# Turning q and k in quarters of the array, and moving a quarter of one block's first product behind the block before it

## The chip, the cores and the metric

The kernel runs on one core of a Trainium2 chip. The metric is the device time of one execution in microseconds (us); a profile of one execution has its own span, which is a little shorter than the time. The engines are named as in the profile: PE is TensorE (PEld its weight loads), DVE is VectorE, ACT is ScalarE, POOL is GpSimd, SP is SyncE, which here only issues transfers.

## What is computed

A retention layer feeds a feed-forward block. From the reference, cut to its core:

```python
for t in range(S):                       # B=4, H=8, S=768, D=64
    state = gamma * state + k[:, :, t] (outer) v[:, :, t]
    y[:, :, t] = scale * q[:, :, t] @ state
x = y.transpose(0, 2, 1, 3).reshape(B * S, H * D)      # 3072 x 512
h = x @ w_in                                            # 512 x 2048
out = (h * sigmoid(1.702 * h)) @ w_out                  # 2048 x 512
```

All is float32, but the weights come in as 64-bit floats, seen by the kernel as pairs of 32-bit words. Turning them into float32 is a part of the work.

## The kernel before, in words

**Retention in chunks.** Time is cut into chunks of 64 steps for two batches at a time, which makes 24 chunks of 128 rows. `turn(j)` turns q and k of chunk j so that the head dimension lies on the partitions. For the first eight chunks it does so on TensorE, with matmuls against the identity (L232) into two PSUM tiles `pt` under the tag "y"; `turned(j)` copies these to SBUF on ACT (L243). For later chunks DVE transposes. `attend(j, f)` (the table calls it `step`) makes the scores of chunk j (L265, into `pa`), the update of the state of chunk f (L275, into `pa`) and the output of f (L284 from the state, L290 from the scores, into `py`). All these are matmuls of 64x64 on quarters of the array, in the order 00, 01, 10, 11 of row half and column half. DVE then does `masked` (L296: scores times mask), `by_state` (called `state` in the table, L301), `output` (`x`, L312) and `updated` (L330, L332); ACT does `decay` (L254) and `aged` (L322).

**The feed-forward block.** The 3072 rows are six blocks (NB) of 512 rows, that is four chunks each. The first product of a block, x by w_in, has 16 column groups of 128, handled as 8 pairs. The second product, by w_out, is `down(m)`: seven partial products (a scheme of the Strassen kind on 2 x 2 sub-blocks: seven products in place of eight, paid for with sums and differences of the operands), each in four units, so 28 units of four matmuls of 128x256 (L488). For blocks 2 to 5 the first product is done in seven as well: `up(d)`, d from 0 to 3, each seven products of four matmuls (L435). Blocks 0 and 1 come while the weights are still being converted, and use the plain eight: `up0(th, p)` for block 0 (eight matmuls of 128x256, L384) and `up1(f)` for block 1 (four matmuls of 128x512, L396). Each is followed by `gate` (a sigmoid on ACT, L356) and `gated` (a multiplication on DVE that frees the PSUM tile, L361).

**The weights.** `Narrow` converts one block of weights: `abs` on ACT (L189), `half` (three DVE operations, L193 to L195) and `rest` (three more, L199 to L204). Blocks 1 to 15 are 128x1024; block 0 is done as two of 128x512 (0a and 0b). Numbers 0 to 7 are w_in, pair by pair, and 8 to 15 are w_out. `fetch` loads them into one of three buffers that take turns (`w7a` and so on in the table). `sums_w2(p)` makes the sums of w_out that the seven products need (L415 to L417), `sums_w2_t3` one more (L420), `sums_w1` and `sums_x` those for `up`, on POOL; `sums_g` the sums of the hidden values (L424 to L426 on DVE, L427 on POOL) after each unit of the third partial product, which is key "y1" in the list `P_`. The fourth partial product reads what L426 writes.

**The order of the work.** TensorE is scheduled by hand: its queue is the order in which the program emits. For the front (blocks 0 and 1, chunks 0 to 7) this is a table of names written out in the kernel, from `k0 table q0` to `gated0.1.3`. Names such as `up0.1.3` and `gate1.5` mean block, row half and pair, or block and column group. `pin` keeps the table's order on the other engines as well; what is not pinned (the sums, for instance) goes where the scheduler puts it. Behind the table follows a loop over the blocks m: `up` for m > 1, then the 28 units of `down(m)`, with the chunks of a later block put `between` at every third unit. `ps` is the PSUM pool, with two buffers under each of the tags "x" and "y"; a unit can start only once the tile that held its buffer has been read.

X1 is the input of block 1. It lies in `W2[:, 6]`, the place that `sums_w2_t3` fills later. The hidden values of block 0 lie in the slots 4 to 6 of W1 and X that the sums for `up` write later.

Of the kernel before, what the change touches and what calls it, by code (L numbers as in the profile page):

```python
# [9 lines left out]
F32 = mybir.dt.float32  # L10
# [18 lines left out]
def kernel(  # L29
# [43 lines left out]
    NP = NFF // 2  # L73
    C4 = 32
    EH = DM // 2
    assert 2 * D == P and HP * P == DM and NC % CB == 0 and B % 2 == 0 and DM == 512 and NFF == 16

    const = ctx.enter_context(tc.tile_pool(name="const", bufs=1))
# [29 lines left out]
    def pin(i):  # L108
        return tc.keep_in_program_order(i) if ordered[0] else i
# [112 lines left out]
    def turn(j):  # L222

        QT[j], KT[j] = home(j, "qT"), home(j, "kT")
        if j < 2 * CB:

            x = QKV.pop(("q", j)), QKV["kn", j]
            TURNED[j] = p = [ps.tile([P, HP, P], F32, name="pt", tag="y") for i in range(2)]
            for n in (1, 0) if j else (0, 1):
                for s in range(HP):  # L230
                    for r in range(2):
                        pe.matmul(p[n][HALF[r], s, :], x[n][:, HP * r + s, :], ident, start=True, stop=True)  # L232
        else:
            for t, name in ((QT[j], "q"), (KT[j], "k")):
                tc.keep_in_program_order(dve.transpose(
                    t.rearrange("p h t -> p (h t)"), QKV.pop((name, j)).rearrange("p h s d -> p (h s d)")))
        if 2 * CB <= j < NCH - 2:
            load(j + 2, "qk")

    def turned(j):  # L240
        p = TURNED.pop(j)
# [148 lines left out]
    def up1(f):  # L390

        p, ab = divmod(f, 2)
        h = ps.tile([P, 2, TH], F32, name="ph", tag="xy"[f % 2])
        for c in range(4):
            w = W1[:, p, 2 * ab + c // 2, c % 2, :]
            pe.matmul(h, w, X1[:, c // 2:4:2, c % 2, :], start=(c == 0), stop=(c == 3))  # L396
        return G[:, p, ab:4:2, :], h


    def sums_w1(p):  # L400
        w = [W1[:, p:p + 2, s] for s in range(7)]
        pool.tensor_add(w[4], w[2], w[3])
        pool.tensor_sub(w[6], w[0], w[2])
        pool.tensor_sub(w[5], w[4], w[0])
        pool.tensor_sub(w[2], w[1], w[5])

    def sums_x():
        pool.tensor_sub(X[:, 4], X[:, 2], X[:, 0])
        pool.tensor_sub(X[:, 6], X[:, 3], X[:, 2])
        pool.tensor_sub(X[:, 5], X[:, 3], X[:, 4])  # L410
        pool.tensor_sub(X[:, 2], X[:, 1], X[:, 5])

    def sums_w2(p):
        w = [W2[:, s, p:p + 2, :] for s in range(7)]
        dve.tensor_sub(w[4], w[1], w[0])  # L415
        dve.tensor_sub(w[5], w[3], w[4])
        dve.tensor_sub(w[1], w[2], w[5])  # L417
# [48 lines left out]
    def down(m):  # L466
# [5 lines left out]

        def keep(name, tag, src):
            kept[name] = one.tile([P, 2, EH], F32, name=name, tag=tag)
            act.activation(kept[name], src, AF.Copy)  # L475

        def put(th, e, a, b):
            o = two.tile([P, 2, EH], F32, name="o")
            dve.tensor_add(o, a, b)  # L479
            (pool if m < NB - 1 else act).dma_start(rows[th, e], o)  # L480

        def part(key, sa, sb, new, last, d, then):
            if d == 0 and new:
                acc[key] = ps.tile([P, 2, EH], F32, name="pd", tag=key[0])
            p0 = acc[key]
            for p in range(2 * d, 2 * d + 2):
                for n in range(2):
                    pe.matmul(p0[:, n, :], g1(m, p, sa)[:, n * P:(n + 1) * P], W2[:, sb, p, :],  # L488
                              start=(new and p == 0 and n == 0), stop=(last and p == NP - 1), skip_group_check=True)
            if d == NP // 2 - 1:  # L490
                then(p0)
# [42 lines left out]
        dve.memset(ones, 1.0)  # L534
        dve.memset(first, 0.0)

    def keep_warm(n):

        for _ in range(n):
            pe.matmul(idle.rearrange("p (a b) -> p a b", a=4), ident, ident[:, None, :].to_broadcast([P, 4, P]),  # L540
                      start=True, stop=True)

    def rows():

# [20 lines left out]
    def late_loads():  # L565
# [10 lines left out]
        "warm2": lambda: keep_warm(2), "warm1": lambda: keep_warm(1)}  # L576
# [15 lines left out]
    units = [0]  # L592
# [17 lines left out]

    begin()
    for name in """
        k0 table q0 warm2 turn0 w0b rows warm1 k1 abs0b q1 turned0 step0 v0 w0a half0b mask turn1 causal
        rest0b masked0 decay0 v1 decay1 abs0a half0a step-0 updated0 turned1 q2 step1 rowd k2 whole w2b
        turn2 w2a x0 k3 aged1 masked1 turned2 v2 rest0a abs2 q3 step-1 updated1 state1 decay2 aged2 step2 q4
        x1 half2 decay3 w3b w3a up0.0.0 masked2 turn3 k4 step-2 v3 q5 rest2 k5 gate0.0.0 turned3 updated2
        gated0.0.0 state2 step3 up0.0.2 masked3 abs3 half3 x2 rest3 turn4 w1b step-3 aged3 gate0.0.2 turned4
        state3 w1a w5b updated3 v5 decay4 k6 abs1 x3 gated0.0.2 q6 turn5 half1 up0.0.3 turned5 up0.1.2 step4  # L620
        aged4 w5a rest1 v4 gate0.0.3 decay5 w6a masked4 turn6 gate0.1.2 abs5 w6b step5-4 gated0.0.3 half5
        rest5 up0.0.1 updated4 turned6 k7 abs6 gated0.1.2 state4 gate0.0.1 w4b up0.1.1 half6 aged5
        gated0.0.1 w8a up0.0.5 rest6 masked5 decay6 w4a q7 up0.1.5 gate0.1.1 x4 gate0.0.5 gated0.1.1
        gated0.0.5 abs4 step6-5 w8b half4 gate0.1.5 state5 updated5 turn7 turned7 aged6 abs8 w9b up0.1.6
        gate0.1.6 x5 v6 masked6 gated0.1.5 step7-6 v7 w9a decay7 up0.1.0 rest4 w7a masked7 abs9 updated6
        state6 x6 gated0.1.6 w7b half8 step-7 state7 up0.1.4 gate0.1.4 abs7 x7 up1.8 rest8 half7 up1.5
        gated0.1.4 gate1.8 gated1.8 w11a rest7 half9 up1.4 gate1.4 w10b gated1.4 w10a w11b up0.0.7 gate0.1.0
        up1.0 gated0.1.0 gate0.0.7 rest9 up1.3 gate1.0 gated1.0 abs10 gated0.0.7 w12a gate1.5 gate1.3 up1.2
        gated1.5 gated1.3 gate1.2 w12b up1.6 gated1.2 gate1.6 abs11 up1.9 gate1.9 half11 rest11 up1.11
        gated1.9 gated1.6 up0.0.4 up0.1.7 abs12 w14b half10 gate0.0.4 rest10 aged7 up0.0.6 gate1.11 updated7  # L630
        gated1.11 gated0.0.4 up1.10 gate0.1.7 w14a half12 gate0.0.6 gated0.1.7 abs14 half14 w13a gate1.10
        gated0.0.6 rest12 w13b up1.7 gate1.7 up1.12 up1.13 gated1.10 gate1.13 rest14 gated1.7 gated1.13
        abs13 half13 gate1.12 w15a up1.15 gate1.15 gated1.15 w15b late_loads up1.14 abs15 gated1.12 up0.1.3
        half15 rest13 rest15 up1.1 gate1.14 gated1.14 gate0.1.3 gate1.1 gated1.1 gated0.1.3
    """.split():
        works[name]()
    ordered[0] = False
# [5 lines left out]
    for m in range(NB):  # L643
        between = []
        if m == 0:
            between = [lambda: turn(2 * CB), lambda: step(2 * CB), lambda: None, lambda: None, lambda: turn(2 * CB + 1)]
        elif m == 1:
            between = [lambda: (decay(2 * CB), load(2 * CB + 1, "v"))] + chunks(2 * CB + 1, 3 * CB)[1:]
        elif 1 < m < NB - 2:
            between = chunks((m + 1) * CB + 1, (m + 2) * CB)  # L650
        elif m == NB - 2:
            between = chunks((m + 1) * CB + 1, NCH - 1) + [lambda: step(None, NCH - 1)]
        if m > 1:
            for d in range(NP // 2):
                up(d)
        for n, unit in enumerate(down(m)):
            unit()
            if m == 0 and n < NP and n % 2:
# [3 lines left out]
            if m == 1 and n % 8 == 3:  # L662
                sums_w1(n // 4)
            if between and n % 3 == 2:
                between.pop(0)()
# [48 lines left out]
```

## Time and profile before

| | |
|---|---|
| time, three runs | 684.38, 684.86, 684.91 us, median 684.86 |
| span of the profiled execution | 682.2 us |
| TensorE clock that was granted, of full speed | 0.999 |
| L488, second products of all blocks (1120, 160 and more records) | 381 to 382 ns each |
| L396, block 1's first product | 128 records, 55.6 us busy |
| L232, the turns | 256 records |
| transfers | 46.55 MB, 217 GB/s over the first 24 us |

A record of L488 is one of two that make up a float32 matmul. The durations of matmuls overlap, since they are pipelined: what one costs is the time from one start to the next. In the front (0 to 158 us) the weights are converted, chunks 0 to 7 are worked through, and both first products run. At 158.5 us the second product of block 0 starts, its third partial product at 173.2 us; the last matmul of the program ends at 678.4 us.

### The profile page before, as it was taken

To read this page: it belongs to the slowest core of one execution; us is meant where nothing else is said; L and a number is where in the kernel's file an instruction comes from. 1 tells how busy PE (TensorE), PEld (TensorE's weight loads), DVE (VectorE), ACT (ScalarE), POOL (GpSimd) and SP (SyncE) were. 2 spreads that over 40 slices of the span, in tenths; PEclk is the share of its full clock that TensorE was granted. 3 is DMA by queue.
4 is the path that set the end of the run, shared out by engine and by line. 5 is a ranking of instruction groups with operands and counts; after the bars stand their busy time and mean duration, and the time that the engine had idled before them with its cause. 6 is when DMAs were issued, how large, how long until landed. Compare 5 with 4: busy or idle time off the path is not lost.

```text
span 682.2 us, 13881 instructions
## 1 busy us (share of the span) xinstructions
PE 669.4 (98%) x5832; PEld 558.1 (82%) x5832; DVE 366.9 (54%) x513; ACT 150.9 (22%) x293; POOL 125.6 (18%) x116
## 2 busy tenths in 40 slices
PE   6899999999999999999999999999999999999997
PEld 4788854756888888888888888888888888888886
DVE  4899984989711843443653443563444372345241
ACT  5764423221000001332000332000333000233000
POOL 3000000000467414000434000245100243000020
PEclk9999999999999999999999999999999999999999
DMA  8886531332222224301333310323310210000001
GB/s 192 243 250 203 155 128 58 123 86 35 48 34 64 62 46 103 57 1 16 73 58 84 53 32 11 75 45 76 74 35 4 51 43 32 16 0 1 16 0 47
DMA packets 140318, 46.55 MB, mean 68 GB/s; under 512 B 131808, under 2 KB 132832, under 8 KB 140256
## 3 DMA queue, kind: packets, MB, share of 16 engines
q1 hardware_dynamic: 136352, 39.10, 24.7%
q0 software_dynamic: 1760, 5.26, 2.0%
q10 hardware_dynamic: 2144, 1.31, 0.6%
q8 instruction: 46, 0.75, 0.4%
q14 instruction: 16, 0.13, 0.1%
HBM read 39.33 MB, written 6.29 MB: 67 GB/s over the span
## 4 chain that ended last, share of the span: by engine, by line
PE 84%; DVE 7%; SPq 5%; DMA 1%; issue 1%; ACT 1%; ACTq 0%
PE pd L488 38%; PE px L435 16%; PE py L435 12%; PE ph L384 6%; SPq L140 4%; PE ph L396 4%; PE pa L265 2%; PE pt L232 2%; PE py L290 2%; PE pa L275 2%; PE py L284 2%; SPq L126 1%; DVE G L425 1%; DMA W<-in_moe_w_out_dram 1%; ACT G L254 1%
## 5 line engine op out<-in xcount | busy, mean ns | idle before, releaser
L488 PE MATMUL pd<-W,G 128*128 128x256 f32 x1120 | 247.4, 381 | 0.4 <-DVE G L426 0.3
L488 PEld LDWEIGHTS pd<-W,G 128*128 128x128 f32 x1120 | 211.3, 190 | 30.3 <-DVE G L426 1.2
L435 PE MATMUL px<-X,W 128*128 128x256 f32 x512 | 119.0, 379 | 0.0
L435 PEld LDWEIGHTS px<-X,W 128*128 128x128 f32 x512 | 97.3, 190 | 13.2
L435 PE MATMUL py<-X,W 128*128 128x256 f32 x384 | 90.7, 379 | 0.0
L435 PEld LDWEIGHTS py<-X,W 128*128 128x128 f32 x384 | 73.0, 190 | 9.9
L384 PE MATMUL ph<-X,W 128*128 128x256 f32 x256 | 57.6, 382 | 0.0
L396 PE MATMUL ph<-W,W 128*128 128x512 f32 x128 | 55.6, 592 | 0.0
L384 PEld LDWEIGHTS ph<-X,W 128*128 128x128 f32 x256 | 48.1, 190 | 8.2 <-issue 1.1
L256 POOL TENSOR_TENSOR kd<-kn_in,cold 128x512 f32<-128x512 f32 x14 | 16.4, 1169 | 186.2 <-PE pa L275 164.5
L396 PEld LDWEIGHTS ph<-W,W 128*128 128x128 f32 x128 | 24.3, 190 | 28.9 <-issue 28.4
L427 POOL TENSOR_TENSOR G<-G 128x512 f32<-128x512 f32 x20 | 29.5, 1482 | 91.8 <-DVE G L426 91.8
L356 ACT ACTIVATE sg<-G 128x512 f32<-128x512 f32 x48 | 30.3, 630 | 51.3 <-DVE G L445 31.0
L361 DVE TENSOR_TENSOR G<-G,sg 128x512 f32<-128x512 f32 x48 | 33.4, 695 | 13.7 <-ACT sg L356 13.7
L296 DVE TENSOR_TENSOR at<-pa,mask 128x512 f32<-128x512 f32 x16 | 11.0, 685 | 53.7 <-PE pa L275 53.7
L488 PE MATMUL pd<-W,W 128*128 128x256 f32 x160 | 35.9, 382 | 1.6 <-DVE G L361 1.3
L324 POOL TENSOR_TENSOR state<-state,whole 128x512 f32<-128x512 f32 x13 | 13.5, 1041 | 126.9 <-DVE state L332 126.7
L488 PEld LDWEIGHTS pd<-W,W 128*128 128x128 f32 x160 | 30.1, 190 | 7.2 <-DVE G L361 2.1
L356 ACT ACTIVATE sg<-ph 128x512 f32<-128x512 f32 x32 | 19.0, 596 | 73.4 <-PE ph L396 30.1
L475 ACT ACTIVATE u<-pd 128x512 f32<-128x512 f32 x6 | 3.6, 597 | 135.5 <-PE pd L488 135.5
L480 POOL DMA_DIRECT2D out_dram<-o x20 | 14.9, 746 | 94.3 <-DVE o L479 94.3
L445 DVE TENSOR_TENSOR G<-py,p 128x512 f32<-128x512 f32 x16 | 11.1, 691 | 38.1 <-PE py L435 38.1
(109 smaller groups left out, 661.9 us busy)
## 6 DMA issues: line engine op xcount, KB each, us to landing
W<-in_moe_w_in_dram SPq DMA_DIRECT2D x12, 512.0 KB, 5.0
v_in<-in_v_dram SPq DMA_DIRECT2D x48, 128.0 KB, 3.1
kn_in<-in_k_dram SPq DMA_DIRECT2D x42, 128.0 KB, 3.2
W<-in_moe_w_out_dram SPq DMA_DIRECT2D x10, 512.0 KB, 3.7
out_dram<-o POOLq DMA_DIRECT2D x20, 256.0 KB, 2.6
q_sq<-in_q_dram SPq DMA_DIRECT2D x256, 16.0 KB, 1.8
k_sq<-in_k_dram SPq DMA_DIRECT2D x256, 16.0 KB, 1.8
G<-in_moe_w_out_dram SPq DMA_DIRECT2D x6, 512.0 KB, 3.9
```

Source lines behind the costliest of these rows:

```text
L140: tc.keep_in_program_order(sp.dma_start(t[r0:r0 + C4, :, n], src[b + n * C4 // D, h0:h0 + HP, t0:t0 + C4, d0:d0 + C4] .rearrange("h p d -> ...
L232: pe.matmul(p[n][HALF[r], s, :], x[n][:, HP * r + s, :], ident, start=True, stop=True)
L256: pool.tensor_mul(KD[j], x, d.to_broadcast([P, H, D]))
L265: pe.matmul(pa[HALF[i], r, 0, s, :], KT[j][HALF[r], s, HALF[i]], QT[j][HALF[r], s, HALF[i]], start=True, stop=True)
L356: pin(act.activation(s, h, AF.Sigmoid, scale=1.702))
L361: pin(dve.tensor_mul(g, h[:, i], s[:, i]))
L384: pe.matmul(h[:, ab], w, X[:, 2 * th + c // 2, c % 2, :], start=(ab == 0 and c == 0), stop=(c == 3), skip_group_check=True)
L396: pe.matmul(h, w, X1[:, c // 2:4:2, c % 2, :], start=(c == 0), stop=(c == 3))
L427: pool.tensor_sub(a[1], a[1], a[0])
L435: pe.matmul(acc[:, u, :], W1[:, 2 * d + u, sa, c, :], X[:, sb, c, :], start=(start and u == 0 and c == 0), stop=(stop and c == 1), skip_gr ...
L480: (pool if m < NB - 1 else act).dma_start(rows[th, e], o)
L488: pe.matmul(p0[:, n, :], g1(m, p, sa)[:, n * P:(n + 1) * P], W2[:, sb, p, :], start=(new and p == 0 and n == 0), stop=(last and p == NP - ...
```

## The change

1. **Turns in quarters.** Each turn becomes 32 matmuls of 64x64 in place of 16 with 128 rows and 128 columns. The two PSUM tiles are now split by row half and not by q and k, so each copy holds a half of both.
2. **A quarter of block 1's first product moves.** MOVED = 1: `up1` is left for 12 of 16 column groups. The last four come after block 0's second product as one `up(3)`, in seven products. For this ACT copies X1 to X, and DVE does the sums for pair 3 and for X.
3. **The table reaches into block 0's second product.** Eight of its 28 units (`down`) and all four `sums_w2` stand in the table, which is written anew from the first to the last name. Once `down` has begun, first-product units take only tag "y".
4. **The end.** The last partial product of the last block is done one column half after the other (`last_part`), so that the first half is added and sent off while the second is still being multiplied.
5. `rows`, the product that spreads the decays, comes ahead of the two warm-up matmuls; a third one is gone.

The diff, cut to its core:

```diff
-            TURNED[j] = p = [ps.tile([P, HP, P], F32, name="pt", tag="y") for i in range(2)]
+            TURNED[j] = p = [ps.tile([P, 2, HP, D], F32, name="pt", tag="y") for i in range(2)]
             for n in (1, 0) if j else (0, 1):
                 for s in range(HP):
-                    for r in range(2):
-                        pe.matmul(p[n][HALF[r], s, :], x[n][:, HP * r + s, :], ident, start=True, stop=True)
+                    for i, r in TWO:
+                        pe.matmul(p[i][HALF[r], n, s, :], x[n][HALF[i], HP * r + s, :], ident[HALF[i], HALF[i]],
+                                  start=True, stop=True)
...
-        for n in (1, 0) if j else (0, 1):
-            pin(act.activation((QT[j], KT[j])[n], p[n], AF.Copy))
+        for i, p in enumerate(TURNED.pop(j)):
+            pin(act.activation(t[:, :, :, HALF[i]], p, AF.Copy))
...
+        def last_part(d, halves={}):
+            n = d // (NP // 4)
+            if d % (NP // 4) == 0:
+                halves[n] = ps.tile([P, EH], F32, name="pd", tag="xy"[n])
+            for p in range(NP // 2 * (d % 2), NP // 2 * (d % 2 + 1)):
+                pe.matmul(halves[n], g1(m, p, 1)[:, n * P:(n + 1) * P], W2[:, 3, p, :], start=(p == 0), stop=(p == NP - 1))
+            if d % 2:
+                o = two.tile([P, 2, EH], F32, name="o")
+                dve.tensor_add(o[:, 0], halves[n], kept["t"][:, n])
+                act.dma_start(rows[0, 1][:, n], o[:, 0])
...
-            args = *args, "x" if n < 3 else "xxyx"[(n - 3) % 4]
+            args = *args, "y" if downs else "x" if n < 3 else "xxyx"[(n - 3) % 4]
+        else:
+            args = *args, "y" if downs else "xy"[args[0] % 2]
...
-            + [(f"1.{f}", up1, f) for f in range(NFF)]:
+            + [(f"1.{f}", up1, f) for f in range(NFF - 4 * MOVED)]:
...
-        if m > 1:
+        if m == 1:
+            for d in range(NP // 2 - MOVED, NP // 2):
+                sums_w1(2 * d, dve)
+                if d == NP // 2 - MOVED:
+                    sums_x(dve)
+                up(d)
+        elif m > 1:
             for d in range(NP // 2):
                 up(d)
-        for n, unit in enumerate(down(m)):
+        for n, unit in enumerate(down(m) if m else second):
+            if m == 0 and n < len(downs):
+                continue
             unit()
-            if m == 0 and n < NP and n % 2:
-                sums_w2(n - 1)
             if m == 0 and NP <= n < 3 * NP // 2:
+                act.activation(X[:, n - NP], X1[:, n - NP], AF.Copy)
                 sums_w2_t3(2 * (n - NP))
```

The new table begins and ends so (a line of "..." stands for the part between):

```
w2a k0 table q0 w2b decay0 rows warm abs2 q1 k1 warm turn0 turned0 step0 mask half2 v0 rowd causal
...
gate0.0.4 w13b up1.9 w14a half12 abs13 gated0.0.4 w14b gate1.6 gate1.9 abs14 gated1.6 gate1.11
rest12 half13 up1.2 gated1.11 down up1.8 gated1.9 gate1.8 half14 w15b w15a late_loads rest14 abs15
down gated1.8 rest13 up0.1.6 half15 rest15 gate0.1.6 down updated7 gated0.1.6 sums1 up1.1 up1.5
gate1.1 sums0 gate1.5 sums3 down gated1.1 gated1.5 up1.7 down down gate1.7 down gated1.7 gate1.2
down sums2 gated1.2
```

More of the change, by code (lines that the diff above doesn't have):

```diff
@@ L75 @@
     EH = DM // 2
+    MOVED = 1
     assert 2 * D == P and HP * P == DM and NC % CB == 0 and B % 2 == 0 and DM == 512 and NFF == 16
@@ L240, in turned @@
     def turned(j):
[L241 to L243 removed]
+        t = G[:, 0:2, j % 2 * 2:j % 2 * 2 + 2, :].rearrange("p n a t -> p n (a t)").rearrange(
+            "p n (s t) -> p n s t", s=HP)
+        for i, p in enumerate(TURNED.pop(j)):
+            pin(act.activation(t[:, :, :, HALF[i]], p, AF.Copy))
     def decay(j):
@@ L388, in up0, with up1 @@
         return [(g1(0, p, 2 + i), i) for i in range(2)], h
-    def up1(f):
+    def up1(f, tag):
         p, ab = divmod(f, 2)
-        h = ps.tile([P, 2, TH], F32, name="ph", tag="xy"[f % 2])
+        h = ps.tile([P, 2, TH], F32, name="ph", tag=tag)
         for c in range(4):
@@ L397, in up1, with sums_w1, sums_x @@
         return G[:, p, ab:4:2, :], h
-    def sums_w1(p):
+    def sums_w1(p, by=pool):
         w = [W1[:, p:p + 2, s] for s in range(7)]
[L402 to L411, printed above, removed]
+        by.tensor_add(w[4], w[2], w[3])
+        by.tensor_sub(w[6], w[0], w[2])
+        by.tensor_sub(w[5], w[4], w[0])
+        by.tensor_sub(w[2], w[1], w[5])
+    def sums_x(by=pool):
+        by.tensor_sub(X[:, 4], X[:, 2], X[:, 0])
+        by.tensor_sub(X[:, 6], X[:, 3], X[:, 2])
+        by.tensor_sub(X[:, 5], X[:, 3], X[:, 4])
+        by.tensor_sub(X[:, 2], X[:, 1], X[:, 5])
     def sums_w2(p):
         w = [W2[:, s, p:p + 2, :] for s in range(7)]
-        dve.tensor_sub(w[4], w[1], w[0])
-        dve.tensor_sub(w[5], w[3], w[4])
-        dve.tensor_sub(w[1], w[2], w[5])
+        pin(dve.tensor_sub(w[4], w[1], w[0]))
+        pin(dve.tensor_sub(w[5], w[3], w[4]))
+        pin(dve.tensor_sub(w[1], w[2], w[5]))
     def sums_w2_t3(p):
@@ L474, in keep @@
             kept[name] = one.tile([P, 2, EH], F32, name=name, tag=tag)
-            act.activation(kept[name], src, AF.Copy)
+            pin(act.activation(kept[name], src, AF.Copy))
         def put(th, e, a, b):
             o = two.tile([P, 2, EH], F32, name="o")
-            dve.tensor_add(o, a, b)
+            pin(dve.tensor_add(o, a, b))
             (pool if m < NB - 1 else act).dma_start(rows[th, e], o)
+        def last_part(d, halves={}):
[8 more added lines that the diff above has]
+                act.dma_start(rows[0, 1][:, n], o[:, 0])
         def part(key, sa, sb, new, last, d, then):
+            if m == NB - 1 and key == "x2":
+                last_part(d)
+                return
             if d == 0 and new:
@@ L535, in begin, with keep_warm @@
         dve.memset(first, 0.0)
[L537 to L541, printed above, removed]
+    def keep_warm():
+        pe.matmul(idle.rearrange("p (a b) -> p a b", a=4), ident, ident[:, None, :].to_broadcast([P, 4, P]),
+                  start=True, stop=True)
     def rows():
@@ L575 @@
         "rowd": lay_rowd, "whole": lay_whole, "late_loads": late_loads,
-        "warm2": lambda: keep_warm(2), "warm1": lambda: keep_warm(1)}
+        "warm": keep_warm}
     for j in range(2 * CB):
@@ L590, with down_unit @@
         works |= {"abs" + name: n.start, "half" + name: n.half, "rest" + name: n.rest}
-    units = [0]
+    units, downs, second = [0], [], down(0)
+    def down_unit():
+        second[len(downs)]()
+        downs.append(0)
+    works["down"] = down_unit
+    for d in range(NP // 2):
+        works[f"sums{d}"] = lambda d=d: sums_w2(2 * d)
     def unit(name, what, *args):
@@ L614 @@
     for name in """
[L615 to L634, printed above, removed]
+        w2a k0 table q0 w2b decay0 rows warm abs2 q1 k1 warm turn0 turned0 step0 mask half2 v0 rowd causal
@@ new lines @@
+        turn1 masked0 w0a rest2 turned1 abs0a step1-0 decay1 w0b abs0b v1 updated0 k2 masked1 whole q2
+        half0a half0b x0 step-1 aged1 state1 turn2 q3 turned2 updated1 k3 w1b x1 w1a decay2 rest0a v2 step2
+        rest0b turn3 masked2 w3a v3 q4 up0.0.2 turned3 k4 abs1 half1 aged2 step3-2 up0.0.0 masked3 gate0.0.2
+        decay3 turn4 state2 w3b updated2 x2 gated0.0.2 rest1 step-3 q5 w5a k5 aged3 w5b decay4 gate0.0.0
+        turned4 updated3 up0.0.1 q6 gated0.0.0 abs3 v4 state3 x3 gate0.0.1 step4 w4a half3 w4b turn5 up0.1.1
@@ new lines @@
+        decay5 gated0.0.1 k6 rest3 abs5 up0.1.3 turned5 half5 w6a abs4 gate0.1.1 rest5 aged4 gate0.1.3 k7 v5
+        w6b masked4 up0.1.0 gated0.1.1 gate0.1.0 gated0.1.3 step5-4 gated0.1.0 half4 turn6 q7 decay6 up0.1.2
+        rest4 turned6 state4 v6 w8a masked5 turn7 up0.1.4 updated4 gate0.1.2 x4 w7a step6-5 abs6 half6
+        gate0.1.4 gated0.1.2 gated0.1.4 turned7 masked6 rest6 up0.0.5 w7b up0.1.5 v7 state5 abs7 decay7
+        aged5 half7 w8b gate0.0.5 abs8 gated0.0.5 up0.0.6 updated5 gate0.0.6 gate0.1.5 x5 rest7 aged6 w10b
@@ new lines @@
+        w9b step7-6 up0.0.7 gated0.0.6 state6 w10a gated0.1.5 x6 masked7 gate0.0.7 half8 up0.0.3 updated6
+        gate0.0.3 rest8 step-7 w11b state7 abs10 w11a up0.1.7 gated0.0.3 x7 w9a gated0.0.7 half10 up1.10
+        up1.3 rest10 up1.4 gate1.10 abs9 gated1.10 half9 abs11 gate1.3 rest9 gate1.4 gated1.3 gated1.4 w12a
+        gate0.1.7 up1.0 aged7 half11 gated0.1.7 up1.6 up1.11 gate1.0 rest11 w12b w13a abs12 gated1.0 up0.0.4
+        gate0.0.4 w13b up1.9 w14a half12 abs13 gated0.0.4 w14b gate1.6 gate1.9 abs14 gated1.6 gate1.11
@@ L645 @@
         if m == 0:
-            between = [lambda: turn(2 * CB), lambda: step(2 * CB), lambda: None, lambda: None, lambda: turn(2 * CB + 1)]
+            between = [lambda: turn(2 * CB), lambda: step(2 * CB), lambda: turn(2 * CB + 1)]
         elif m == 1:
@@ L652 @@
             between = chunks((m + 1) * CB + 1, NCH - 1) + [lambda: step(None, NCH - 1)]
-        if m > 1:
+        if m == 1:
[5 more added lines that the diff above has]
+        elif m > 1:
             for d in range(NP // 2):
                 up(d)
-        for n, unit in enumerate(down(m)):
+        for n, unit in enumerate(down(m) if m else second):
+            if m == 0 and n < len(downs):
+                continue
             unit()
-            if m == 0 and n < NP and n % 2:
-                sums_w2(n - 1)
             if m == 0 and NP <= n < 3 * NP // 2:
+                act.activation(X[:, n - NP], X1[:, n - NP], AF.Copy)
                 sums_w2_t3(2 * (n - NP))
-            if m == 1 and n % 8 == 3:
+            if m == 1 and n % 8 == 3 and n // 4 < NP - 2 * MOVED:
                 sums_w1(n // 4)
```

## The prediction

> **What bounds the kernel now.** I read the page first, then the waits of TensorE, the busy time by stretch, and the timelines of TensorE and VectorE.
>
> ```profile
> span 682.2 us, 13881 instructions
> ...
> PE 669.4 (98%) x5832; PEld 558.1 (82%) x5832; DVE 366.9 (54%) x513; ACT 150.9 (22%) x293; POOL 125.6 (18%) x116
> ```
>
> TensorE is busy for 98% of the span. Its waits, all of them:
>
> ```profile
> PE idle L540 <- POOL ident masks.py:199: 3.9, 1, 3.9
> PE pa L265 <- issue: 1.4, 1, 1.4
> PE pa L265 <- DVE state L330: 1.3, 1, 1.3
> PE pd L488 <- DVE G L361: 1.3, 1, 1.3
> ```
>
> From 24 to 157 us it never waits. But in that stage VectorE is nearly full as well (columns after the stretch and its length: PE, PEld, DVE, ACT, POOL):
>
> ```profile
> 24.00:86.00 62.00, 61.96 (x1075) 53.65 (x1076) 58.22 (x77) 34.50 (x87) 0.00 (x0) 1.00 0.72 203
> 86.00:158.40 72.40, 71.15 (x206) 38.76 (x204) 58.92 (x74) 20.18 (x32) 1.04 (x1) 1.00 0.30 95
> ```
>
> So a shorter TensorE queue is worth something in the front only as far as VectorE, which converts the weights, can keep up. Two timelines give the prices, TensorE's
>
> ```profile
> 27.56 1.09 PE L232 MATMUL pt<-ident,kn_in 128*64 128x128 f32 x16
> 28.49 1.04 PE L232 MATMUL pt<-ident,q_in 128*64 128x128 f32 x16
> 29.46 0.69 PE L275 MATMUL pa<-v_in,G 64*64 64x64 f32 x32
> 29.98 0.65 PE L284 MATMUL py<-G,state 64*64 64x64 f32 x32
> 98.54 20.76 PE L396 MATMUL ph<-W,W 128*128 128x512 f32 x48
> ```
>
> (two records are one matmul; start to start counts) and VectorE's, one block of weights:
>
> ```profile
> 41.41 0.68 DVE L193 TENSOR_SCALAR W<-W 128x1024 f32<-128x1024 f32 x1
> 42.12 0.69 DVE L194 TENSOR_SCALAR W<-W 128x1024 uint32<-128x1024 uint32 x1
> 42.85 1.23 DVE L195 SCALAR_TENSOR_TENSOR W<-W,W 128x1024 uint32<-128x1024 uint32 x1
> 44.11 0.70 DVE L199 TENSOR_SCALAR W<-W 128x1024 uint32<-128x1024 uint32 x1
> 44.84 1.23 DVE L200 SCALAR_TENSOR_TENSOR W<-W,W 128x1024 f32<-128x1024 uint32 x1
> 46.10 1.23 DVE L204 TENSOR_TENSOR W<-W 128x1024 f32<-128x1024 f32 x1
> ```
>
> A half costs 2.58 us start to start and a rest 3.12 (5.84 when adjacent); other 128x512 operations follow each other every 0.60, or 0.72 if one reads the one before.
>
> [...] The trace agrees for L284: sixteen 64x64 matmuls in 0.47 us. [...] Here the first four records of 512 columns take 3.71 us where warm ones take 0.43 each, and speed comes some 4.5 us after the first matmul. [...] Here L425 takes 1.64 instead of 0.69 us beside L427.
>
> **Part 1, the turns.** Before: 16 matmuls of 128 columns, 0.93 + 0.97 = 1.90 us per chunk. After: 32 of 64x64 in L284's quarter order, 2 x 0.48 = 0.97 (bounds 0.93 to 1.9, should only two quarters overlap). Over 8 chunks TensorE sheds 7.4 us. ScalarE's two copies stay 0.60 each, but each now holds q and k, so neither starts before the whole turn.
>
> **Part 2, the moved product.** Four up1 units (x48 records = six units in 20.6 us, 3.45 each) leave: 13.8. Seven products of four matmuls come after block 0: 7 x 1.73 (the chain's px and py pieces) = 12.1. TensorE sheds 1.7 us. Its operands cost VectorE 8 sums, 4.8 us, in a stretch where it was nearly idle (0.69 of 10 us at 190:200). The sum that waits for block 0's very last product (w5) lies behind one 0.7 us addition and is done 1.5 us later; up reads it only in its third product, 3.45 us on. Hidden. The four copies of X1 are 0.6 each on ScalarE, 28% busy, but one matters (part 3).
>
> **Part 3, the front as reordered.** TensorE alone would give 7.4 + 1.7 us, the 1.3 us wait and the tail. The order of the changed kernel's instructions on each engine says VectorE becomes the limit, so I walk it. *Start:* rows heads TensorE's queue; its row landed 3.9 us after its issue at 2.70, so 6.6 instead of the 3.86 of the warm-up. Six cold records, the last one or two fast, end near 11.7; turn0 12.7, two copies 14.0, step0 14.5, masked0 at 14.6. Block 2's half is done by then (its four loads, 1.57 MB, land by 9 to 10 us, judged from 2.40 MB by 12 us). *VectorE from masked0 to rest7:* rest2, six further blocks and the two small ones (3.12 + 6 x 5.70 + 2 x 3.30 + 0.4 for adjacency = 44.3), 7 masked, 6 updated, 5 state and x (14.3), 9 gated (5.7): 64.3 us without a gap I can find, so rest7 ends at 78.9. *TensorE* needs it for up0.0.7; then four up0 (14.0), six up1 (20.7), step-7 (1.5): up0.0.4 ends at 115.1. ScalarE has queued a copy of X1 ahead of its gate: copy, gate, abs13 (1.18), gate1.6 follow, and gated1.6 starts at 118.3, where VectorE has stood idle about 3.6 us in all (its own queue was through half12 at 114.1). *VectorE again:* 4 gated, 7 halves and rests (20.5), updated7, gated0.1.6: 24.1, to 142.4. Once down units are out, every up takes a "y" buffer, of two: up1.5 waits for gated0.1.6, up1.7 for gated1.1, which stands behind three sums_w2 (6.1 us): 149.2. Then up1.7 (3.45) and four down units (7.05): the third product of block 0 starts at 159.8. TensorE alone would be there at 153.4, so 6.4 us of what it sheds is lost. In the kernel before, it starts at 173.2.
>
> **Part 4, after that point.** Before, 505.2 us passed from 173.2 to the last matmul (678.4). Added: 12.1 for the seven products, 0.6 for the pa of chunk 8, which stood earlier before. And VectorE: before, 14 operations from the first output addition to the last L426 took 12.4 us, and the fourth product waited 0.3 us. Now six more stand between (three of sums_w2(6), gated1.2, one L422, the mask of chunk 8): 6 x 0.65 = 3.9. Some of this meets slack: I take 2.6 us more waiting (bounds 0 and 3.9). Sum 520.5: the last matmul ends at 680.3.
>
> **Part 5, the tail.** Before, last matmul to end was 3.8 us:
>
> ```profile
> 678.43 0.69 DVE L479 TENSOR_TENSOR o<-pd,t 128x512 f32<-128x512 f32 x1 [4.99 <-PE pd L488]
> ```
>
> Half of it now comes early; the last addition is 128x256 (0.41, as L361 at that size) and its transfer half as large: 3.1 us (an estimate; 2.8 to 3.5).
>
> **Sum.** 680.3 + 3.1 = 683.4 us of span. The median lies 2.66 above the profiled span (684.86 - 682.2): 686.0, about 1 us over the kernel before.
>
> **Rivals.** *A, faster: the pairing is a little better than I walk.* If the array warms earlier and the gates cost no gap (2 us), and the six operations meet slack (2.6): 681.4. For it: the reversed bounds above, and a kernel before in which TensorE waited nowhere over 130 us. Against: rest7 follows from VectorE's own queue. *B, TensorE stays the limit:* 153.4 + 505.2 + 12.1 + 0.6 + 3.1 + 2.66 = 677.1. For it: 98% busy. Against: VectorE's sum from half2 to gated1.1, 134 us, plus the 10.5 us behind it, from its start near 10 ends near 155 even without one gap, 1.6 later than TensorE alone. *C, slower by more:* at 22 us TensorE stood 1.4 us waiting for nothing the profile shows, with the transfer engines 97% busy; the turns now hold twice the instructions there, and VectorE's chain no longer has idle time to absorb it. Two such stops, or a turn at 1.4 us instead of 0.97 with its lag passed on: about 3 us, 689.
>
> **How the numbers follow.** Forecast 0.50, A 0.27, B 0.08, C 0.15. No change by the 0.2% bound is 683.5 to 686.2, so the forecast lies at its upper edge and splits: about half of it same, most of the rest slower. Faster 0.32, same 0.25, slower 0.43. Range 680.5 (A with its slack) to 689.0 (C); B is left out.
>
> **What would show it.** Right: turns of about 0.97 us; TensorE waiting near 37 us for L205 (rest1), and before up1.5 and up1.7 for L363; VectorE over 95% busy from 15 to 110 us; a wait of some 3 us in the fourth product for L428; the third product starting near 160. Wrong: no wait of TensorE between 100 and 155 us, or turns of 1.9 us. If rows starts well before 6.6 us, everything up to 160 shifts by that.

## The result and the profile after

The changed kernel takes 691.37 us (median of four runs, 690.71 to 693.54) against 684.85: the ratio is 1.0102, with a 95% interval of 1.0079 to 1.0126. It is slower by 1.0%, and outside the range of the prediction (680.5 to 689.0). Its runs also lie further apart than those of the kernel before (2.8 us against 0.5). The profiled execution, 691.6 us of span, is the slowest of the four; the other spans are 688.8 to 689.9.

The page's first lines (span, and busy time of each engine):

```profile
span 691.6 us, 14451 instructions
...
PE 666.0 (96%) x6110; PEld 559.2 (81%) x6110; DVE 375.5 (54%) x526; ACT 154.6 (22%) x300; POOL 124.9 (18%) x112
```

TensorE did shed work: 666.0 us instead of 669.4. What grew is its waiting. From its waits (engine, tile and line, releaser: total, times, longest):

```profile
PE rows L562 <- DMA G<-in_row_decay_dram: 8.7, 1, 8.7
PE pt L232 <- issue: 3.4, 1, 3.4
PE ph L398 <- DVE g L363: 2.6, 1, 2.6
...
PE pa L277 <- issue: 1.3, 1, 1.3
...
PE pd L505 <- DVE W L428: 0.3, 1, 0.3
PE py L292 <- issue: 0.2, 1, 0.2
```

The first matmul comes at 8.7 us instead of 3.9, and three stops marked "issue" (TensorE waits there for nothing that the profile shows) add up to 4.9 us. The busy time by stretch, for the two stretches that were shown of the kernel before (stretch, length, busy PE, PEld, DVE, ACT, POOL; clock, share of the transfer engines, GB/s):

```profile
24.00:86.00 62.00, 56.76 (x1195) 49.52 (x1196) 55.74 (x81) 36.42 (x97) 0.00 (x0) 0.97 0.70 189
86.00:158.40 72.40, 68.65 (x427) 41.89 (x426) 67.30 (x85) 21.97 (x36) 1.04 (x1) 0.98 0.40 121
```

In the first stretch TensorE is idle for 5.2 us and VectorE for 6.3: neither of them is the limit all the time. The timeline of TensorE shows where (start, duration, line, tiles, count, idle time ahead):

```profile
8.67 2.04 PE L562 MATMUL rows<-G 1*128 1x512 f32 x2 [8.67 <-DMA G<-in_row_decay_dram]
10.64 3.78 PE L556 MATMUL idle<-ident 128*128 128x512 f32 x4
14.35 1.13 PE L232 MATMUL pt<-ident,q_in 64*64 64x64 f32 x32
15.26 1.08 PE L232 MATMUL pt<-ident,kn_in 64*64 64x64 f32 x32
...
29.23 0.55 PE L232 MATMUL pt<-ident,kn_in 64*64 64x64 f32 x20
33.17 0.39 PE L232 MATMUL pt<-ident,kn_in 64*64 64x64 f32 x10 [3.40 <-issue]
...
34.37 4.97 PE L386 MATMUL ph<-X,W 128*128 128x256 f32 x16
...
51.63 0.65 PE L232 MATMUL pt<-ident,kn_in 64*64 64x64 f32 x32
52.09 0.65 PE L232 MATMUL pt<-ident,q_in 64*64 64x64 f32 x32
...
170.11 5.47 PE L505 MATMUL pd<-W,X 128*128 128x256 f32 x24
183.57 2.00 PE L505 MATMUL pd<-W,W 128*128 128x256 f32 x8 [0.26 <-DVE W L428]
...
206.12 1.89 PE L437 MATMUL px<-X,W 128*128 128x256 f32 x8
```

TensorE stands still in the middle of turn3, between two matmuls of one loop. VectorE feels the late start and the stop:

```profile
18.32 0.69 DVE L298 TENSOR_TENSOR G<-pa,mask 128x512 f32<-128x512 f32 x1 [3.64 <-PE pa L267]
36.49 0.69 DVE L194 TENSOR_SCALAR W<-W 128x1024 f32<-128x1024 f32 x1 [3.18 <-ACT W L190]
40.51 0.69 DVE L298 TENSOR_TENSOR G<-pa,mask 128x512 f32<-128x512 f32 x1 [1.34 <-PE pa L277]
...
126.42 0.69 DVE L363 TENSOR_TENSOR W<-ph,sg 128x512 f32<-128x512 f32 x1 [2.71 <-ACT sg L358]
...
688.13 0.42 DVE L493 TENSOR_TENSOR o<-pd,t 128x256 f32<-128x256 f32 x1 [2.82 <-PE pd L490]
```

The gap at 36.49 is the stop, passed on: on ScalarE, block 1's magnitudes (L190) stand behind the copies of turn3 (L245), and these started only at 34.36, after the turn. The gap at 40.51 follows an up0 product at 34.37 that takes 4.97 us (granted clock 0.50 from 34 to 36 us). In the kernel before, the same product takes 3.62, or 3.45 from its start to the next one's:

```profile
150.10 3.62 PE L384 MATMUL ph<-X,W 128*128 128x256 f32 x16
```

### The profile page after: what moved, and what is told of

Read it like the earlier page. It is cut to its first block, busy times and chain, and to the rows that moved or that the text cites. A ratio compares the mean times of both kernels' runs of the same rounds, so it can differ in the third digit from the quotient of the medians.

```text
span 691.6 us, 14451 instructions
## 1 busy us (share of the span) xinstructions
PE 666.0 (96%) x6110; PEld 559.2 (81%) x6110; DVE 375.5 (54%) x526; ACT 154.6 (22%) x300; POOL 124.9 (18%) x112
## 4 chain that ended last, share of the span: by engine, by line
PE 86%; SPq 6%; DVE 3%; DMA 2%; issue 2%; ACT 0%; POOL 0%; ACTq 0%; POOLq 0%
PE pd L505 36%; PE px L437 17%; PE py L437 13%; PE ph L386 8%; SPq L141 6%; PE ph L398 3%; PE pa L267 2%; PE py L292 1%; PE pa L277 1%; PE py L286 1%; PE pt L232 1%; PE pd L490 1%; DMA G<-in_row_decay_dram 1%; DVE G L427 1%; DMA W<-in_moe_w_out_dram 1%
## 5 line engine op out<-in xcount | busy, mean ns | idle before, releaser
L505 PE MATMUL pd<-W,G 128*128 128x256 f32 x1088 | 240.5, 381 | 0.4 <-DVE G L428 0.3
L505 PEld LDWEIGHTS pd<-W,G 128*128 128x128 f32 x1088 | 205.5, 190 | 29.2 <-DVE G L428 1.2
L437 PE MATMUL px<-X,W 128*128 128x256 f32 x544 | 126.6, 379 | 0.0
L437 PEld LDWEIGHTS px<-X,W 128*128 128x128 f32 x544 | 103.5, 190 | 13.9
L437 PE MATMUL py<-X,W 128*128 128x256 f32 x408 | 96.4, 379 | 0.0
L437 PEld LDWEIGHTS py<-X,W 128*128 128x128 f32 x408 | 77.6, 190 | 10.4
L398 PE MATMUL ph<-W,W 128*128 128x512 f32 x96 | 44.2, 615 | 3.6 <-DVE g L363 2.6
L398 PEld LDWEIGHTS ph<-W,W 128*128 128x128 f32 x96 | 18.6, 196 | 26.5 <-issue 24.1
L358 ACT ACTIVATE sg<-ph 128x512 f32<-128x512 f32 x28 | 16.5, 595 | 60.2 <-PE ph L398 34.2
L461 DVE TENSOR_TENSOR G<-py,vv 128x512 f32<-128x512 f32 x17 | 11.8, 692 | 27.4 <-ACT vv L458 27.4
```

Of the source, the lines that this page charges most:

```text
L358: pin(act.activation(s, h, AF.Sigmoid, scale=1.702))
L437: pe.matmul(acc[:, u, :], W1[:, 2 * d + u, sa, c, :], X[:, sb, c, :], start=(start and u == 0 and c == 0), stop=(stop and c == 1), skip_gr ...
L461: dve.tensor_add(a[3], z, vv)
```

## The experiments

The kernel before was run beside every set, with medians of 684.85 to 685.67 us, so the ratios are what is to be compared.

| kernel | us | ratio to before | interval |
|---|---|---|---|
| changed kernel | 691.37 | 1.0102 | 1.0079 to 1.0126 |
| changed, rows behind turn0 | 689.82 | 1.0060 | 1.0039 to 1.0081 |
| changed, turns of before | 692.02 | 1.0094 | 1.0078 to 1.0110 |
| changed, both | 690.48 | 1.0073 | 1.0051 to 1.0095 |
| changed, rows behind turn0, quarters from chunk 4 | 688.17 | 1.0030 | 1.0013 to 1.0048 |
| changed, thin early weights | 686.30 | 1.0008 | 0.9999 to 1.0017 |
| before, quarters alone | 694.27 | 1.0128 | 1.0100 to 1.0156 |
| before, moved product alone | 688.11 | 1.0037 | 1.0020 to 1.0055 |
| before, last product in halves alone | 685.73 | 1.0003 | 0.9991 to 1.0015 |
| before, moved product, halves, retabled | 682.38 | 0.9959 | 0.9945 to 0.9972 |
| the same, quarters from chunk 5 | 691.28 | 1.0089 | 1.0075 to 1.0103 |

**The quarters alone.** The two hunks of turn and turned put into the kernel before, nothing else:

```diff
-            TURNED[j] = p = [ps.tile([P, HP, P], F32, name="pt", tag="y") for i in range(2)]
+            TURNED[j] = p = [ps.tile([P, 2, HP, D], F32, name="pt", tag="y") for i in range(2)]
...
-                        pe.matmul(p[n][HALF[r], s, :], x[n][:, HP * r + s, :], ident, start=True, stop=True)
+                        pe.matmul(p[i][HALF[r], n, s, :], x[n][HALF[i], HP * r + s, :], ident[HALF[i], HALF[i]],
+                                  start=True, stop=True)
```

> The kernel before with the quarter turns alone. TensorE sheds 8 x 0.93 = 7.4 us, VectorE has 58.2 of 62 us to do from 24 to 86, so at most some 4 us can come through. Theory 2: stops marked issue of 2 to 4 us appear in the first 40 us, where before had 0.3 and 1.4, and take the gain away: 683 to 687. Rival (quarters are harmless): the stops stay at 1.7 us and the kernel takes 681 to 683.

Measured: 9 us slower, worse than either theory. The waits of TensorE in this kernel:

```profile
PE pt L232 <- issue: 4.1, 1, 4.1
...
PE pa L277 <- issue: 3.4, 1, 3.4
PE py L286 <- issue: 2.3, 1, 2.3
...
PE py L292 <- issue: 1.1, 1, 1.1
```

The stops add up to 10.9 us, against 1.7 before. And a stop costs more than its own length. The stretch around and behind the end of the 3.4 us stop (20.03 to 23.41), with its granted clock (the number after POOL), and the product that runs there:

```profile
22.59:32.83 10.24, 8.76 (x121) 7.49 (x121) 7.49 (x10) 5.41 (x21) 0.00 (x0) 0.50 0.81 209
```

```profile
27.32 6.42 PE L386 MATMUL ph<-X,W 128*128 128x256 f32 x16 [0.66 <-DVE X L314]
```

Here the granted clock is 0.50 and the product takes 6.35 us from start to start, instead of 3.45. In all, the clock stands at half for 20.5 us of this kernel's front, and never in the front of the kernel before. In this stop it fell when TensorE had stood for 2.6 us (20.03 to 22.59). In the last kernel of the table, a stop of 1.64 us is followed by a product of 5.41 us, at a clock of 0.50.

**The turns of before in the changed kernel.** The reverse of the two hunks above, in the changed kernel.

> The changed kernel with the turns of before: 16 matmuls of 128 columns for q or k instead of 64 of 64x64, and one copy for each of q and k. All else as changed. Theory 2 (twice the instructions in the turns starve TensorE's instruction supply while the transfers are at their fullest): the stops marked issue shrink to under 1.5 us in all, against 1.3 + 3.4 + 0.2, and the wait of VectorE at 36 us goes; TensorE has 7.4 us more to do but waited longer than that in the front, so 686 to 690 us. Rival (the stop has nothing to do with the turns, and the quarters are a gain): the 3.4 us stop stays, and the kernel takes 692 to 699.

Measured: no stop marked "issue" is left at all, as theory 2 says. But the time, 692.02 us, is outside its 686 to 690, at the edge of the rival's range. It did not fall (1.0094 against 1.0102, intervals that overlap): the turns take back on TensorE about what the stops had cost, and the third product of block 0 starts at 168.75. So the stops are those of the quarters; but the quarters, at 0.93 us saved a turn, have about paid for them here, and with neither the kernel is still 0.9% behind the kernel before.

**The start.** One entry of the table moved:

```diff
-        w2a k0 table q0 w2b decay0 rows warm abs2 q1 k1 warm turn0 turned0 step0
+        w2a k0 table q0 w2b decay0 warm abs2 q1 k1 warm turn0 rows turned0 step0
...
```

> The changed kernel with one entry moved: rows, the matmul that waits for the row, stands behind turn0 in TensorE's queue instead of ahead of the warm-up. Theory 1 (the start: the row lands at 8.7 us and holds the warm-up back): the warm-up starts at 3.9 and is over by 7.7, turn0 follows q and k at 8 to 10, masked0 starts near 14.6 instead of 18.3, and the kernel takes 691.4 - 3.7 = 687.7 us, if the stops of TensorE behind it stay. Theory 2 (instruction supply): the 3.4 us stop in turn3 is there again, and of the 9.7 us only the first 3.7 come back. Rival (the table itself is slow, and the start is hidden by later waits): 690.5 to 692.

```profile
PE idle L556 <- POOL ident masks.py:199: 3.9, 1, 3.9
...
PE pt L232 <- issue: 2.6, 1, 2.6
```

The warm-up starts at 3.88 and masked0 at 14.52 instead of 18.32: theory 1 holds for the start. Of this 3.8 us, 0.4% of the time comes back (some 2.9 us by the ratios, whose intervals just touch), and the stop in turn3 is there again, at 2.6 us. The time lies 2.1 us above the 687.7 expected; these runs spread over 5 us.

With the old turns as well:

> The changed kernel with both undone: the turns of before, and rows behind turn0. No stop marked issue is left over 0.5 us (as in the changed kernel with old turns), and masked0 starts near 15.5 instead of 18.4 (rows behind turn0 gave 14.5, a turn of before is 0.9 longer). Theory (start and stops together are what the prediction missed, but the turns give back what the stops cost): the third product of block 0 starts at 168.8 - 2.9 = 165.9, and the kernel takes 692.0 - 2.9 = 689 us (688 to 690). Rival (the two faults overlap fully, or the longer turns cost nothing on VectorE's path): 692, or 686 and less.

Measured 690.48, half a microsecond above the range; masked0 at 15.21, no stop left, and the third product at 166.92 instead of 165.9. Most of the 1.0 us that is missing is a wait of VectorE for block 1's magnitudes (1.43 us at 30.66). Undoing both faults at the price of the old turns leaves the kernel 0.7% slower than before.

**The stops themselves.** They are not spread at random. Counting TensorE's records from the first, a stop comes after 221, 348 and 475 of them in the changed kernel; after 221, 348, 857 and 1112 with the quarters alone; after 725, 980 and 1236 in the last kernel of the table. The distances are 127, or 254 to 256, or 509. The 1.4 us stop of the kernel before comes after 346; its other one, of 0.3 us after 104, does not fit these distances. A record is one weight load and one matmul (the page counts as many PEld as PE), so 127 records are 254 instructions. The transfer queue named "instruction" (q8) moves packets of 16 KB. In the whole changed kernel these are

```profile
q8 instruction: 48, 0.79, 0.5%
```

or one for every 254.6 of the 12220 weight loads and matmuls. In the kernel before, 46 packets go with 11664 of them, one for every 253.6. Three answers of the transfer view of the changed kernel, for 20.0 to 20.5, 23.5 to 24.0 and 30.5 to 31.0 us:

```profile
q8 instruction: 1, 0.02, 11.6%
...
q8 instruction: 1, 0.02, 16.2%
...
q8 instruction: 1, 0.02, 14.2%
```

Each shows one packet, and is followed by the end of one stop, 2.1 to 2.7 us later: 22.58, 26.24 and 33.17. So I take a packet for a block of about 254 instructions, and a stop for the wait for the next block; this is inferred from these counts and times. From 26.24 to 29.77 the changed kernel used up one block in 3.5 us; the next one was ready 6.9 us after the former had begun. A block of 64x64 matmuls alone would last 127 x 0.015 = 1.9 us, an estimate from the 0.47 us that 32 records of L284 take.

**Thin early weights.** Is it the load of the transfer engines that makes a block late?

```diff
     def fetch(i):
         x = raw(i).rearrange("p (n two) -> p n two", two=2)
+        if i < 8:
+            pin(sp.dma_start(x.rearrange("p (c f) two -> p c f two", c=2)[:, :1, :32], SRC[i][:, :1, :32]))
+            return
...
         dve.memset(first, 0.0)
+        for x in (RAWS[2], RAWS[0], RAWS[1]):
+            pin(dve.memset(x.bitcast(F32).rearrange("p (n k) -> p n k", n=2)[:, :, 64:], 1.0))
```

> The changed kernel whose first eight weight transfers (w0a to w3b, 512 KB each) move 1/16 of their bytes, the rest of the three raw tiles being filled once by VectorE at the start: the weights are wrong, the work on all compute engines is that of the changed kernel but for three fills of some 2 us on VectorE, which had nothing to do there. Theory (instruction blocks are fetched by the same loaded transfer engines): the stops marked issue, 4.9 us in all, fall below 1 us, and q8's packets come at shorter intervals; the row lands near 6.6 instead of 8.7 (theory 1). VectorE's gaps before masked0 and at 36 us shrink, the third product starts near 161 to 164, and the kernel takes 682 to 685.5. Rival (the stops are set by TensorE's rate of instructions alone): over 3 us of stops stay and the kernel takes 688 or more.

```profile
PE rows L567 <- DMA G<-in_row_decay_dram: 6.4, 1, 6.4
...
PE pa L280 <- issue: 0.4, 1, 0.4
PE pt L235 <- issue: 0.4, 1, 0.4
...
PE py L295 <- issue: 0.2, 1, 0.2
PE pa L270 <- issue: 0.2, 1, 0.2
```

This kernel leaves out 15/16 of these weights, so what it computes is not the reference's result; it is there for its times. The stops come after the same 221, 348 and 475 records, but are 0.41, 0.20 and 0.37 us long, and the blocks follow each other after 3.66 and 3.92 us instead of 3.66 and 6.93. A fourth, of 0.17 us, comes after 855. Their sum, 1.2 us, is just above what was expected, and so is the time (686.3 against 682 to 685.5). By these two runs, both the load and TensorE's own rate count. The shortest interval, 3.66 us, appears in both kernels, with the transfer engines 39 and 47% busy over it; the longest, 6.93 us, had them 79% busy. The row, too, lands earlier, at 6.4 instead of 8.7. GpSimd issues it and SyncE the weights; from issue to landing it took 3.6 us instead of 5.8. That the row and the instruction blocks are held up by the weight transfers is read from these two runs. VectorE has 0.9 us of gaps left between masked0 and rest7, where the changed kernel has 6.0, and the third product starts at 162.77. That is 7.3 us earlier than in the changed kernel's profile: 2.2 us of start and 5.1 of gaps. By the ratios these two causes, the row and the late blocks with the slow products behind them, are worth 0.94% (6.4 us): nearly all of what the changed kernel loses against the kernel before.

**Quarters where long matmuls stand between.** The changed kernel with rows behind turn0 and this:

```diff
-            TURNED[j] = p = [ps.tile([P, 2, HP, D], F32, name="pt", tag="y") for i in range(2)]
+            if j < 4:
+                TURNED[j] = p = [ps.tile([P, HP, P], F32, name="pt", tag="y") for i in range(2)]
...
+            else:
+                TURNED[j] = p = [ps.tile([P, 2, HP, D], F32, name="pt", tag="y") for i in range(2)]
...
```

> The changed kernel with rows behind turn0, the turns of before for chunks 0 to 3 (with the first 40 us of full transfer engines and no long matmul between), quarters for chunks 4 to 7, where up0 products of 3.5 us stand between the turns. Theory (the stops come where TensorE passes 127 matmuls faster than the next block arrives, which needs short matmuls alone): no stop over 0.5 us, TensorE sheds 3.7 us against old turns throughout, of which VectorE's queue lets through a part: 686 to 689. Rival (quarters stop TensorE wherever they stand): stops of 2 us or more in turns 4 to 7, 690 or more.

As expected: no stop, 688.17 us, 0.43% less than with old turns throughout.

**The moved product alone.**

```diff
-            + [(f"1.{f}", up1, f) for f in range(NFF)]:
+            + [(f"1.{f}", up1, f) for f in range(NFF - 4 * MOVED)]:
...
-        if m > 1:
+        if m == 1:
+            for d in range(NP // 2 - MOVED, NP // 2):
+                sums_w1(2 * d, dve)
+                if d == NP // 2 - MOVED:
+                    sums_x(dve)
+                up(d)
+        elif m > 1:
```

> The kernel before with the moved product alone: the last four up1 units and their gates leave the table, the rest of the table and its turns stay, and seven products with their sums follow block 0's second product. TensorE: 13.8 us out of the front, 12.1 + 0.6 us in behind it, and the front keeps up to a few us of the 13.8 as waits for VectorE, whose queue there shrinks by 2.4 us only. The theory that the moved product is harmless: 684 to 687. Rival (the moved product is what costs): 688 or more.

Measured 688.11, just on the rival's side of the border. TensorE's waits and VectorE's timeline say why:

```profile
PE pd L489 <- DVE W L205: 3.5, 1, 3.5
...
PE pa L266 <- DVE kT L236: 1.2, 1, 1.2
```

```profile
105.18 0.69 DVE L362 TENSOR_TENSOR G<-ph,sg 128x512 f32<-128x512 f32 x1 [2.07 <-ACT sg L357]
...
108.56 0.69 DVE L362 TENSOR_TENSOR G<-ph,sg 128x512 f32<-128x512 f32 x1 [1.16 <-ACT sg L357]
112.00 0.69 DVE L362 TENSOR_TENSOR G<-ph,sg 128x512 f32<-128x512 f32 x1 [2.74 <-ACT sg L357]
116.46 0.69 DVE L194 TENSOR_SCALAR W<-W 128x1024 f32<-128x1024 f32 x1 [3.77 <-ACT W L190]
```

TensorE comes to its last blocks earlier and now waits for VectorE's last conversion, while VectorE itself has stood idle for 10 us before, while block 10, fetched at 96 us, and block 11, at 97, stand queued behind gates.

**The last product in halves alone.**

> The kernel before with the last product in two halves alone. The last matmul stays where it was; the last addition is 128x256 instead of 128x512 and its transfer half as large: span and time 0.3 to 0.7 us shorter, 684.2 to 684.9. Rival (the first half's addition or its transfer gets in the way of the second): 685.2 or more.

Measured 685.73, a ratio of 1.0003: no difference to be seen. The time itself lies in the rival's range, but the kernel before took 685.67 beside it, so neither theory is settled. In its profile the end comes 3.5 us after the last matmul instead of 3.8; such a gain is below what these runs resolve.

**A version that beats both.** The moved product and the halves, with the turns and the start of before, and one stretch of the table reordered (its core):

```diff
-        rest9 up1.3 gate1.0 gated1.0 abs10 gated0.0.7 w12a gate1.5 gate1.3 up1.2 gated1.5 gated1.3 gate1.2
-        w12b up1.6 gated1.2 gate1.6 abs11 up1.9 gate1.9 half11 rest11 up1.11 gated1.9 gated1.6 up0.0.4 up0.1.7
-        abs12 w14b half10 gate0.0.4 rest10
...
+        abs10 rest9 up1.3 gate1.0 gated1.0 gated0.0.7 half10 w12a gate1.5 gate1.3 w12b up1.2 rest10 abs11
+        gated1.5 gated1.3 w13a w13b gate1.2 half11 up1.6 gated1.2 gate1.6 rest11 w14b w14a up1.9 gate1.9 abs12
+        up1.11 gated1.6 gated1.9 half12 up0.0.4 up0.1.7 gate1.11 rest12 w15a w15b
...
```

> The kernel before with the moved product and the last product in halves, turns and start of before, and one stretch of the table in another order: blocks 10 and 11 are converted as soon as they have landed, which fills VectorE's 10 us of gaps between 103 and 116 us, and blocks 13 to 15 are fetched and converted earlier. Theory (in the moved product alone, what TensorE shed was lost to VectorE's last conversion, 3.5 us of waiting for L205, and to a transpose behind it, 1.2 us): both waits go, the third product starts at 166.9 - 4.7 = 162.2, and the kernel takes 688.1 - 4.7 - 0.3 = 683.1 us, 2 under the kernel before. Rival (VectorE's earlier conversions hold the gates back, and TensorE waits for buffers): 687 or more.

```profile
PE pa L266 <- issue: 1.4, 1, 1.4
...
PE pd L504 <- DVE W L427: 1.2, 2, 0.9
```

Measured 682.38, 0.41% faster than the kernel before (interval 0.28 to 0.55%) and 1.4% below the changed one by the ratios. Both waits are gone; the third product starts at 158.36 instead of 173.21, 14.85 us earlier: nearly all of the 13.8 us of the four units and of the 1.3 us wait of the kernel before comes through. It gives 13.1 back behind that, for the seven products (12.1) and 0.9 us more in waits for L427.

**The same with quarters from chunk 5.**

> The same with quarters for the turns of chunks 5 to 7 only, behind 50 us, where long matmuls stand between the turns. Theory (quarters are worth 0.93 us each where no block of instructions is late): no stop over 0.5 us behind 45 us, TensorE sheds up to 2.8 us more, of which VectorE lets through a part: 681 to 683. Rival (stops come with the quarters there too): a stop of 2 us or more in turns 5 to 7, 685 or more.

My theory lost: 691.28, 8.9 us more.

```profile
40.54 0.40 PE L240 MATMUL pt<-ident,q_in 64*64 64x64 f32 x13
44.01 0.56 PE L240 MATMUL pt<-ident,q_in 64*64 64x64 f32 x19 [3.07 <-issue]
44.51 8.86 PE L399 MATMUL ph<-X,W 128*128 128x256 f32 x32
...
58.29 0.56 PE L305 MATMUL py<-G,v_in 64*64 64x64 f32 x20 [1.64 <-issue]
58.79 5.41 PE L399 MATMUL ph<-X,W 128*128 128x256 f32 x16
```

That long matmuls stand somewhere between the turns is not enough. Here scores, states, outputs and turn follow each other, so that one whole block, from record 598 on, holds only 64x64 matmuls and is used up in 2.1 us (38.85 to 40.95, by counting records back), while the next comes 5.2 us after it began. In the changed kernel's order no stop comes behind 34 us. The stops of 3.07, 1.64 and 1.24 us (the last in turn7), and the slow products behind the first two (8.86 instead of 7.17 us, 5.41 instead of 3.62, by the same line of the kernel before) come to 5.95 + 1.7 + 1.8 = 9.4 us, against 2.8 that TensorE shed. That accounts for 6.6 of the 8.7 us by which the third product starts later (167.04 against 158.36). Another 0.9 were lost by 25 us, behind a wait of 2.1 us for VectorE, after which half a turn took 1.76 us instead of 0.92 (granted clock 0.86 from 20 to 25 us); the rest was not traced.

## Why the prediction was wrong

**Part 1, the turns: the price was right.** 0.46 + 0.58 = 1.04 us in the lines of 51.63 and 52.09, 0.97 predicted: 16 ns a record of 64 columns, where a record of L396 takes 434 ns for 512 columns (55.6 us for 128 records), or 54 for 64. So the quarters did run side by side. But the part priced a matmul by its time in the array alone. Twice as many instructions in half the time is a price too, on the supply of instructions, and it is the step that failed: the term was put at nothing in "64.3 us without a gap I can find". VectorE's own work from masked0 to rest7 was 64.4 us (88.75 - 18.32, less the gaps), exactly the sum; the gaps were 0.86, 3.18, 1.34, 0.24 and 0.37 us, 6.0 in all, and with thin weights 0.9. That the 0.86 is the first stop, the 3.18 the stop of turn3, and the 1.34 the slow product behind it (4.97 instead of 3.62 us), is read from the order of ScalarE and TensorE; that they go when blocks come sooner is shown.

**Part 3, the start: failed by 3.7 us** (masked0 at 18.32, not 14.6). 2.1 us are the row: "its row landed 3.9 us after its issue" was taken over from a kernel whose first 512 KB load is issued at 2.31, 0.4 us ahead of the row; here w2a's is issued at 0.81, 1.9 us ahead, and the row took 5.8. The kernel with thin weights shows this piece: row at 6.42, 6.6 predicted. The other 1.6 us are there even then (masked0 at 16.08): the first six records take 5.7 us instead of 5.1, and turn0 takes 0.91 for its first half instead of 0.48. The prediction had the last of the six records fast already, but 6.6 us after the first matmul those of turn0 still came at half their usual rate, where the kernel before was at its usual rate after some 4.5 (its turn0 takes 1.35 and 0.97 us for its halves, a later turn 0.93 and 0.97). The clock column reads 1.00 there in both kernels, so the slow start shows in these times alone. Why it lasted longer was not tried.

**Part 3 behind rest7: right.** From rest7 to the third product 80.9 us were predicted and 81.4 measured, with the 3.6 us gap behind ScalarE's copy (2.71 + 0.82), the waits before up1.5 and up1.7 (2.6 and 0.2; 2.6 and 1.9 with thin weights), and the "y" buffers as their cause. One thing was not foreseen and did no harm here: behind the 2.6 us wait the granted clock fell once more (0.50 from 153.0 to 156.4 us),

```profile
152.35 5.37 PE L398 MATMUL ph<-W,W 128*128 128x512 f32 x8 [2.63 <-DVE g L363]
```

and up1.5 took 5.20 us instead of 3.50 with thin weights. That used up the second wait, so up1.7 came 7.32 us after up1.5 in both. But starting 9.8 us late, the third product came at 170.1 instead of 159.8, only 3.1 earlier than in the kernel before.

**Part 2 and part 4.** The moved product took 206.12 to 218.21 = 12.09 us without a wait: right. "I take 2.6 us more waiting" in the fourth product was mis-sized: the wait was 0.26 us, as before, so nothing was added. All in all 12.8 us were added behind the third product, 15.3 predicted.

**Part 5: right in kind, 0.4 us too short** (3.5 from the last matmul to the end, 3.1 predicted). Its saving, 0.3 us, cannot be told from none.

**The sum.** 683.4 us of span were predicted for 691.6: +3.7 (start), +6.0 (gaps), +0.1 and +0.5 (walk), -2.5 (fourth product), +0.4 (tail) are 8.2. The profiled execution lies 2.2 above the median, and the distance from span to time was 1.9 instead of 2.66, which leaves 5.3 of the 5.4 us of the miss. The 2.66 was a slip: it set the median against the span of a run that itself took 684.16 us, and from that run's span to its own time it is 1.96.

**The rivals.** C named the cause, a TensorE that waits for nothing the profile shows, and saw it in the kernel before, at 1.4 us; it was given 3 us and a chance of 0.15. It was too small because it counted stops and not the things behind them: how many instructions a block holds, how long a block takes to come, and the slow products behind a stop (4.97 us instead of 3.62). A and B needed a front without those stops. The forecast's own figure, 686.0, is met within 0.3 us by the kernel with thin weights, where neither of the two causes acts in full, but partly by luck: its third product still comes 3.0 us late, and the 2.5 us of waiting that did not come make up for most of that.

**The signs.** Turns of about 0.97 us and the waits before up1.5 and up1.7 came. The others did not: no wait for L205 near 37 us, VectorE busy for 88% from 15 to 110 us instead of over 95, 0.26 us in the fourth product, and a third product at 170.

What stays open: when a block is requested and how many are held ahead, which these runs do not show, and why TensorE stayed slow for so long at the start, where the last 1.6 us are lost.

## What to carry to other kernels

Price an instruction twice: by its time in the array, and as 1 of about 254 in a block. Here the next block was ready 3.7 to 6.9 us after the one before had begun; where small matmuls used up a block faster than that (in 2.1 to 3.5 us), the time saved in the array was lost again (7.4 us were to be saved by the quarters alone, and their stops took 10.9), and behind a stop the granted clock could fall to 0.50. Count records between stops marked "issue": equal distances (127 records here), and a packet on q8 2.1 to 2.7 us before each stop ended, pointed to the supply of instructions. And work taken off TensorE pays only after the partner's queue is re-read: the same moved product cost 0.4% in one order of VectorE's work and gained 0.4% in another (there with the halves, which alone made no difference).

## What was not expected of the hardware

- TensorE's stops lie 127 records, or multiples of about that, apart, and q8 moves one 16 KB packet for about as many (48 for 6110 records). In the changed kernel work resumes 2.1 to 2.7 us after a packet. The ends of neighbouring stops lie 3.66 us apart at the least (transfer engines 39 and 47% busy) and 6.93 at the most (79%).
- Behind a stop of 1.6 to 3.4 us products took 1.4 to 2.8 us longer; with the 3.4 us stop of the quarters alone, the granted clock was 0.50 for 10.2 us. A wait for data can do the same (2.6 us in the changed kernel, clock 0.50 for 3.4 us), but does not always: with thin weights the product behind the same wait took 3.50 us (granted clock of that run 0.999), and the 1.4 us stop of the kernel before left the clock at 1.00.
- A 2 KB transfer, issued at 2.7 us, took 3.9 us from issue to landing where the first 512 KB load was issued at 2.31 us, and 5.8 where one was issued at 0.81 and another at 2.75; 3.6 where these two were thin.
